# An event table of a transformer-block kernel: row maxima, one activation and the last attention results moved to other times, queues and banks

## The chip, the cores and the metric

The kernel runs on one core of a Trainium2 chip. The metric is device time in microseconds (us) of one execution, from the first to the last instruction and the little that lies around them; a kernel's time is the median of its runs. All arithmetic that the output depends on is done in the kernel.

## The reference

A block with adaptive layer norms works on x of 2048 rows and 576 columns. It has windowed attention with 32 heads of 18 columns, a token mixer with shifted rows, and an MLP of width 4608. Cut to what matters:

```python
def _A_ref(x, wqkv, wo):                       # H = 32, Dh = 18, W = 256
    q, k, v = ...                              # x @ wqkv, split into heads
    scores = jnp.einsum("bhqd,bhkd->bhqk", q, k) * (Dh ** -0.5)
    mask = (idx[:, None] - idx[None, :] >= 0) & (idx[:, None] - idx[None, :] < W)
    p = _softmax(jnp.where(mask, scores, -1e9), axis=-1)
    return (p @ v).reshape(B, S, D) @ wo       # written short

def _B_ref(x, w1, w2, w3, w4):
    h = _gelu(_layernorm(x) @ w1)
    hs = jnp.concatenate([four column groups of h, shifted by +1, -1, +2, -2 rows]) @ w2
    x1 = x + hs
    return x1 + _gelu(_layernorm(x1) @ w3) @ w4

h = _layernorm(x) * (1 + ca) + sa              # sa, ca, ga, sb, cb, gb = silu(c) @ w_mod
x = x + ga * _A_ref(h, A_wqkv, A_wo)
h = _layernorm(x) * (1 + cb) + sb
return x + gb * _B_ref(h, B_w1, B_w2, B_w3, B_w4)
```

## The kernel before

**How the order of work is set.** The class Kern does not issue its work in loops. Each piece (a function such as mtr or wom) is recorded with a time by at(t, f); build (line 1354) sorts all pieces by these times and runs them in that order, and what a piece issues lands at the end of its engines' queues. The times are only a table that orders; the chip knows nothing of them. Each engine works through its own queue in order, and an instruction waits on semaphores for what it reads and for the buffer that it writes. So a piece that is given another time stands at another place in every queue that it uses. Tiles of a pool rotate under a tag: a new tile under a tag waits until the old one's readers are done. The PSUM tags are s0 to s3 (one bank each) and m0 and m1 (two banks each).

**Stages.** qkv (projections, with q, k and v stored to DRAM), attention, mixing, mlp, each overlapping the next. A product of full precision is made of three fp32r products: an operand is split into a high part (a cast, mostly on ScalarE) and a low part (a subtraction on VectorE or GpSimd).

**Attention, head by head.** tm(h) = TA + 13 h turns heads into times; n counts 32 pairs (head groups), and u counts 16 rounds of two n, n = 2u and 2u+1. For each n, load (line 483) brings Q and K by SyncE (lines 489 and 493). mx (line 513) multiplies queries by keys once to get the row maxima; red takes them on VectorE (line 537) into the tile m. Then come three pieces that the change touches. mtr (line 543) transposes m on TensorE into the PSUM tile mt; mev (line 547) casts it on ScalarE into ms; mst (line 551) sends ms by two small DMAs into rows 108 and 109 of Q, so that the second product of queries and keys, xm (line 562, tiles X, banks s0 and s1, two matmul lines 568 and 570) comes out with the maxima subtracted. ex (line 582) takes its exponential on ScalarE into P.

**The value burst.** Once a round, av (line 593) multiplies P by V in a burst of about 230 small matmuls (line 607) into banks s2 and s3. avs (line 610) copies both banks on ScalarE, otr (line 614) transposes the copies back into s2 and s3 (tiles ot), onm (line 619) normalises on VectorE (reciprocal, line 624, and product, line 625), and ost (line 627) stores o.

**The output projection** goes by 16 row blocks t, one in each round from the sixth on: orow loads the block, otT transposes it (tiles pa, pb), otev splits it into T (casts on ScalarE, lines 678 and 679; low parts on VectorE, 680 and 681), wom multiplies by Wo in two halves (line 692), woe adds x (696), ln1 takes statistics (130 to 132), ln1n normalises in two steps (707 and 708), ln2 takes statistics again, ln2n (line 717) makes xn on ScalarE, and st1 to st3 store. wotile sets the times of blocks 0 to 9; last(te), with te = tm(34.07), those of blocks 10 to 15 and of the last round's results. The last burst, av15, has the time tm(34.05), or te - 0.26.

**The mixer's start.** mixing begins at te + 0.01, beside these last blocks: w1split casts W1 (lines 849 and 850) with low parts of slices 1 and 3 on VectorE (852, 854) and the others on GpSimd; tr transposes xn (ptm, line 895), tev splits it into xT (902 to 905), and w1mm makes the first products pg (line 916). w2split casts W2 on ScalarE (872).

Of the kernel before, what the change touches and what calls it, by code (L numbers as in the profile page):

```python
# [8 lines left out]
F32 = mybir.dt.float32  # L9
# [10 lines left out]
P = 128  # L20
# [13 lines left out]
class Kern:  # L34
# [34 lines left out]
    def at(self, t, f, *a):  # L69
        self.ev.append((t, (lambda: f(*a)) if a else f))  # L70
# [382 lines left out]
    def attention(self, t1, t2, TA, HU, LX=2.05):  # L453
        nc, at, ps = self.nc, self.at, self.ps
        X, M = {}, self.rowm
        tm = lambda h: TA + HU * h
# [84 lines left out]
                    nc.vector.tensor_reduce(out=m[:, c + s:c + s + 1], in_=pm[:, s, 320 - w:320], axis=mybir.AxisListType.X, op=ALU.max, negate=True)  # L541

        def mtr(n):
            pt = X["mt", n] = ps.tile([16, P], F32, tag="s3", name=f"mt{n}")
            nc.tensor.transpose(pt, X["m", n], self.ident)

        def mev(n):
# [3 lines left out]
        def mst(n):  # L551
            ms, Q = X["ms", n], X["Q"][n % 4]
            for r in range(2):
                nc.scalar.dma_start(Q[108 + r:109 + r].bitcast(F32), ms[:, 64 * r:64 * r + 64].bitcast(F32))

        BANKS = [[(0, 0), (5, 320)], [(-2, 0), (1, 192)], [(-4, 0), (2, 64), (6, 384)], [(-3, 0), (3, 128), (7, 448)], [(-1, 0), (4, 256)]]

# [170 lines left out]
        def wotile(t, h, b0=2):  # L728
            at(tm(h - 0.2), orow, t)
            at(tm(h + 0.42), otT, t, b0)  # L730
            at(tm(h + 0.43), otev, t)
            at(tm(h + 0.77), wom, t, 0, b0)
            at(tm(h + 0.92), woe, t, 0)
            at(tm(h + 1.15), wom, t, 1, b0)
            at(tm(h + 1.16), ln1, t, 0)
            at(tm(h + 1.30), woe, t, 1)
            at(tm(h + 1.31), ln1, t, 1)
            at(tm(h + 1.95), st1, t)
            at(tm(h + 1.712), ln1n, t)
            at(tm(h + 1.714), ln2, t)  # L740
            at(tm(h + 2.05), ln2n, t)
            at(tm(h + 2.1), st2, t)
            at(tm(h + 2.35), st3, t)

        N = 32
        for n in range(N):
            at(max(t1 + .5 + n * .01, tm(n - (0.98 if n < 12 else 0.86))), load, n)
            for j in range(2):
                at(max(t1 + .6, tm(n - 0.3 + 0.5 * j)), qs, n, j)
                for bb in range(4):  # L750
                    th = n + (4 * j + bb) / 8
                    at(tm(th), mx, n, j, bb)
                    at(tm(th + .06), red, n, j, bb)
                    if n in (1, 2):
                        at(tm(th + .01), self.warm, 2, "s3")
                at(max(t2 + .01, tm(n + LX - (0.77 if n < 12 else 0.6) + 0.47 * j)), ks, n, j)
                for k in range(5):
                    th = n + LX + (5 * j + k) / 10
                    at(tm(th), xm, n, j, k)
                    at(tm(th + .03), ex, n, j, k)  # L760
            hm = n + (1.47 if n % 2 else 1.16)
            at(tm(hm), mtr, n)
            at(tm(hm + .005), mev, n)
            at(tm(hm + .006), mst, n)
        for u in range(16):
            h = 2 * u + LX + 2
            if u == 15:
# [14 lines left out]
        for t in range(10):  # L782
            wotile(t, 12.4 + 2 * t)

        def last(te):
            for r in range(2):
                at(te + 5.0 + .01 * r, avs, 15, r)
                at(te + 9.9 + .1 * r, otr, 15, r)
                at(te + 11.4 + .1 * r, onm, 15, r)
            at(te + 13.3, ost, 15)  # L790
            for t, b0, o, a, w0, w1 in ((10, 0, -8.0, 5.02, 7.9, 11.6), (11, 2, .05, 13.6, 15.95, 17.65), (12, 2, 13.4, 19.75, 21.15, 23.2),
                                        (13, 2, 21.2, 32.1, 33.75, 35.45), (14, 2, 29.2, 37.55, 38.9, 40.6), (15, 2, 42.5, 49.85, 51.5, 53.2)):
                at(te + o, orow, t)
                at(te + a, otT, t, b0)
                at(te + a + .02, otev, t)
                for hf, w in ((0, w0), (1, w1)):
                    at(te + w, wom, t, hf, b0)
                    at(te + w + 2.05, woe, t, hf)
                e = te + w1 + 2.1
                for d, f in ((.3, ln1), (1.0, st1), (3.0, ln1n), (4.9, ln2), (5.5, st2), (7.5, ln2n), (9.5, st3)):  # L800
                    at(e + d, f, t)
# [600 lines left out]
```

## Time and profile before

| what | value |
|---|---|
| median of 3 runs | 1792.72 us (1791.35 to 1794.88) |
| profiled execution | 1794.32 us, span of its instructions 1792.5 us |
| mean granted TensorE clock over the span | 0.982 |
| busy share of the span | TensorE 94%, its weight loads 86%, VectorE 62%, GpSimd 50%, ScalarE 39% |
| 240 to 380 us, attention without a full output projection | TensorE 125.21 of 140 us, ScalarE 68.14 |
| 640 to 657 us, the last round | TensorE 14.34 of 17 us, ScalarE 11.56 |
| 657 to 690 us, last burst and the mixer's start | TensorE 27.16 of 33 us, clock 0.90 |

The profile is of one execution. In its rows PE is TensorE's matmuls, PEld its weight loads, DVE VectorE, ACT ScalarE, POOL GpSimd, SP SyncE; ACTq and SPq are the issues of DMAs from those engines' queues, which hold the queue up though they are not counted as busy. A row of a timeline gives start, duration, engine, line, operation, output <- inputs, the count where neighbours are drawn together, and in brackets how long the engine was idle before and what ended that. A row of a window gives its bounds and length, then busy time (and count) of PE, PEld, DVE, ACT, POOL, the granted clock, the DMA share and GB/s. A row of waits gives the waiting engine, tile and line, what released it, then total, count and longest. A row of groups gives busy total and mean ns of one, then the idle time before.

### The profile page before, as it was taken

How to read it: one execution, taken by the hardware profiler on the slowest of the kernel's cores; microseconds unless marked ns; L12 is line 12 of the kernel's file. 1: busy time of each engine (PE TensorE's matmuls, PEld its weight loads, DVE VectorE, ACT ScalarE, POOL GpSimd, SP SyncE). 2: the span in 40 equal slices, each digit the busy share in tenths (PEclk: the TensorE clock that was granted, in tenths of full speed). 3: DMA queues.
4: the chain of work that ended last, by engine and by line, in shares of the span. 5: the costliest groups of instructions: out<-in, count | busy, mean ns of one | idle time of the engine just before them, and what ended most of it. 6: DMA issues, size and time to landing. Idle time of an engine off the chain costs nothing.

```text
span 1792.5 us, 33622 instructions
## 1 busy us (share of the span) xinstructions
PE 1687.1 (94%) x13369; PEld 1535.6 (86%) x13369; DVE 1103.0 (62%) x1887; ACT 707.3 (39%) x1211; POOL 898.8 (50%) x837
## 2 busy tenths in 40 slices
PE   7999998999999989988799999999979999999998
PEld 5888887888989879988588999999878999999997
DVE  6544354666767636666666666666675666666664
ACT  3222144454545554444333433333433333344331
POOL 4222347445454533454766555556644556655550
PEclk9999998999999999999899999999989999999999
DMA  8854553546455446544422222211233211122211
GB/s 257 275 183 154 176 159 103 145 135 172 130 153 163 145 138 204 192 159 141 162 75 63 63 63 62 59 45 52 62 126 96 63 52 49 56 63 62 62 45 53
DMA packets 156499, 206.77 MB, mean 115 GB/s; under 512 B 19316, under 2 KB 87924, under 8 KB 155768
## 3 DMA queue, kind: packets, MB, share of 16 engines
q1 hardware_dynamic: 153720, 203.19, 36.9%
q8 instruction: 106, 1.74, 0.4%
q10 hardware_dynamic: 2624, 1.45, 0.3%
q14 instruction: 49, 0.40, 0.1%
HBM read 143.76 MB, written 60.56 MB: 114 GB/s over the span
## 4 chain that ended last, share of the span: by engine, by line
PE 73%; DVE 6%; DMA 5%; POOL 5%; issue 4%; ACT 4%; SPq 1%; ACTq 1%; POOLq 0%; DVEq 0%
PE d L1256 24%; PE qk L331 6%; PE X L568 3%; PE v L369 3%; PE mx L519 3%; PE wo L692 3%; PE av L607 3%; PE pg L916 2%; PE X L570 1%; PE w L965 1%; DVE W L1114 1%; DMA wmf<-in_w_mod_dram 1%; DMA or<-od 1%; DMA wf<-in_B_w_dram 1%; ACT avs L612 1%
## 5 line engine op out<-in xcount | busy, mean ns | idle before, releaser
L1256 PE MATMUL d<-W,G 128*128 128x288 f32 x3456 | 507.7, 297 | 12.5 <-DVE acc L1264 9.2
L1256 PEld LDWEIGHTS d<-W,G 128*128 128x128 f32 x3456 | 489.2, 189 | 34.9 <-DVE acc L1264 10.3
L1264 DVE TENSOR_TENSOR acc<-d,acc 128x576 f32<-128x576 f32 x288 | 216.9, 754 | 205.6 <-PE d L1256 203.2
L1094 POOL TENSOR_TENSOR wf<-wf 128x384 f32<-128x384 f32 x140 | 147.0, 1071 | 339.8 <-DMA wf<-in_B_w_dram 333.8
L585 ACT ACTIVATE P<-X 128x512 f32<-128x512 f32 (+4 forms) x320 | 177.8, 572 | 202.3 <-PE X L570 160.8
L537 DVE TENSOR_REDUCE m<-mx 128x2 f32<-128x640 f32 x144 | 117.8, 819 | 109.0 <-PE mx L523 108.5
L568 PE MATMUL X<-QD,KS 128*128 128x64 f32 (+2 forms) x704 | 146.2, 300 | 10.8 <-ACT P L585 9.8
L1106 POOL TENSOR_TENSOR W<-wf,W 128x768 fp32r<-128x768 f32 x70 | 152.9, 2207 | 1.2 <-ACT W L1100 1.2
L519 PE MATMUL mx<-KD,QS 128*128 128x320 f32 (+4 forms) x512 | 144.7, 342 | 7.4 <-DVE m L537 3.2
L1233 DVE TENSOR_TENSOR G<-U,G 128x512 fp32r<-128x512 f32 x108 | 88.5, 819 | 99.0 <-ACT G L1226 99.0
L499 POOL TENSOR_SCALAR QS<-QD,rowm 128x512 fp32r<-128x512 f32 x128 | 87.9, 701 | 111.6 <-DMA QD<-qd 56.4
L1224 ACT ACTIVATE U<-U 128x512 f32<-128x512 f32 x108 | 68.3, 632 | 178.3 <-DVE U L1209 178.2
L1224 ACT ACTIVATE C<-C 128x512 f32<-128x512 f32 x36 | 22.8, 632 | 286.4 <-DVE C L1209 286.4
L568 PEld LDWEIGHTS X<-QD,KS 128*128 128x128 f32 x704 | 108.6, 194 | 19.5 <-ACT P L585 16.1
L331 PE MATMUL qk<-hT,Wqk 128*128 128x512 f32 x462 | 109.3, 396 | 1.2 <-DVE qs L345 1.2
L506 POOL TENSOR_SCALAR KS<-KD,rowm 128x768 fp32r<-128x768 f32 (+1 forms) x128 | 108.5, 863 | 0.0
L1120 POOL TENSOR_TENSOR wf<-wf,gb 128x1152 f32<-128x1152 f32 x35 | 103.4, 2955 | 6.9 <-DMA wf<-in_B_w_dram 6.9
L331 PEld LDWEIGHTS qk<-hT,Wqk 128*128 128x128 f32 x462 | 86.4, 188 | 23.4 <-DVE qs L345 1.6
L519 PEld LDWEIGHTS mx<-KD,QS 128*128 128x128 f32 x512 | 93.5, 194 | 14.1 <-issue 5.3
L1135 POOL TENSOR_TENSOR W<-wf,W 128x1152 fp32r<-128x1152 f32 x35 | 96.8, 2766 | 6.9 <-ACT W L1129 6.9
L1100 ACT CAST W<-wf 128x1152 fp32r<-128x1152 f32 x70 | 90.2, 1318 | 20.5 <-DMA wf<-in_B_w_dram 10.4
L570 PE MATMUL X<-Mk,identr 128*128 128x256 f32 (+2 forms) x320 | 96.6, 302 | 0.0
(787 smaller groups left out, 3211.3 us busy)
## 6 DMA issues: line engine op xcount, KB each, us to landing
wf<-in_B_w_dram SPq DMA_DIRECT2D x35, 576.0 KB
wf<-in_B_w_dram SPq DMA_DIRECT2D x140, 128.0 KB
KD<-kd SPq DMA_DIRECT2D x72, 216.0 KB
QD<-qd SPq DMA_DIRECT2D x96, 144.0 KB
wf<-in_B_w_dram SPq DMA_DIRECT2D x140, 64.0 KB
qd<-qs SPq DMA_DIRECT2D x16, 512.0 KB
kd<-qs SPq DMA_DIRECT2D x16, 512.0 KB
vd<-Vst SPq DMA_DIRECT2D x16, 312.0 KB
```

Source lines behind the costliest of these rows:

```text
L331: nc.tensor.matmul(po, W[:, a, fs], H[:, c, :], start=(n == 0), stop=(n == 13))
L506: nc.gpsimd.tensor_scalar(t[:, b0:, r], src[:, b0:], M[:, 2 + r:3 + r], 0.0, op0=ALU.mult, op1=ALU.add)
L519: nc.tensor.matmul(pm[:, s, 320 - 64 * nb:320], lhs, K[:, j, 64 * (i + 5 - nb):64 * (i + 5)], start=True, stop=merged(n, j, bb))
L537: nc.vector.tensor_reduce(out=m[:, c:c + 2], in_=pm[:, :, 0:320], axis=mybir.AxisListType.X, op=ALU.max, negate=True)
L568: nc.tensor.matmul(px[:, c:c + q1 - q0], K[:, b + 4].rearrange("p r k -> p (r k)"), Q[:, j, q0:q1], start=(i == 0), stop=False)
L570: nc.tensor.matmul(o, self.identr, mv, start=False, stop=True)
L585: nc.scalar.activation(p[:, lo:], X["px", n, j, k][:, lo:], AF.Exp, scale=SCALE)
L1094: nc.gpsimd.tensor_tensor(out=WF[:, o], in0=WF[:, a], in1=WF[:, b], op=ALU.subtract)
L1106: eng.tensor_tensor(out=W[:, s0:s1, 3:5, :], in0=WF[:, 1 + s0:1 + s1, 0:2], in1=W[:, s0:s1, 0:2, :].bitcast(F32), op=ALU.subtract)
L1120: nc.gpsimd.tensor_tensor(out=R4, in0=R4, in1=gb.unsqueeze(1).to_broadcast([P, 2, D]), op=ALU.mult)
L1256: nc.tensor.matmul(po, G[:, g, ta, b, ts], W[:, w, b, cs], start=(n == 0), stop=(n == 5))
L1264: nc.vector.tensor_tensor(out=a, in0=po, in1=a, op=ALU.add)
```

## The change

Only places in the event table, one PSUM tag and one DMA queue change; what is computed stays as it was.

1. mtr of odd n (that is, the second of a round) stands under tag s0 instead of s3, and at n + 1.105 instead of n + 1.47: right behind the value burst instead of behind the avs copies.
2. mst issues its two DMAs from SyncE instead of ScalarE, and has the time hm + 0.14 instead of hm + 0.006, where hm is mtr's time.
3. ln2n of blocks 0 to 9 has h + 1.86 instead of h + 2.05: among the exponentials behind the burst instead of behind the avs copies.
4. In last, the results of the last round (avs, otr, onm, ost) come at te + 0.1, 0.35, 0.55 and 4.0 instead of te + 5.0, 9.9, 11.4 and 13.3; block 10's otT and otev come at te - 1.1, ahead of av15, instead of te + 5.02, and its two halves of wom at te + 0.25 and 0.5 instead of 7.9 and 11.6. Its later steps follow from these, 11.1 earlier.

```diff
 def mtr(n):
-    pt = X["mt", n] = ps.tile([16, P], F32, tag="s3", name=f"mt{n}")
+    pt = X["mt", n] = ps.tile([16, P], F32, tag="s0" if n % 2 else "s3", name=f"mt{n}")
...
-        nc.scalar.dma_start(Q[108 + r:109 + r].bitcast(F32), ms[...])
+        nc.sync.dma_start(Q[108 + r:109 + r].bitcast(F32), ms[...])
...
-    at(tm(h + 2.05), ln2n, t)
+    at(tm(h + 1.86), ln2n, t)
...
-    hm = n + (1.47 if n % 2 else 1.16)
+    hm = n + (1.105 if n % 2 else 1.16)
     at(tm(hm), mtr, n)
     at(tm(hm + .005), mev, n)
-    at(tm(hm + .006), mst, n)
+    at(tm(hm + .14), mst, n)
...
-    at(te + 5.0 + .01 * r, avs, 15, r)
-    at(te + 9.9 + .1 * r, otr, 15, r)
-    at(te + 11.4 + .1 * r, onm, 15, r)
-at(te + 13.3, ost, 15)
-for t, b0, o, a, w0, w1 in ((10, 0, -8.0, 5.02, 7.9, 11.6), ...
+    at(te + .1 + .01 * r, avs, 15, r)
+    at(te + .35 + .05 * r, otr, 15, r)
+    at(te + .55 + .05 * r, onm, 15, r)
+at(te + 4.0, ost, 15)
+for t, b0, o, a, w0, w1 in ((10, 0, -8.0, -1.1, .25, .5), ...
```

ScalarE's queue before, in the round of the twelfth burst (av11), from the first exponential behind the burst; ms25 are the row maxima of n = 25, P24 the exponentials of n = 24, xn6 the result of row block 6, QD1 the Q tile that ms goes to:

```order
L585 ACTIVATE P24_0_1_7489<-X24_0_1_7485 128x512
L585 ACTIVATE P24_0_2_7510<-X24_0_2_7500 128x512
L585 ACTIVATE P24_0_3_7524<-X24_0_3_7513 128x512
L612 COPY avs11_0_7528<-av11_0_7356 128x512
L612 COPY avs11_1_7530<-av11_1_7357 128x512
L717 ACTIVATE xn6_7540<-h6_7462,c6rs_7467 128x576
L549 CAST ms25_7544<-mt25_7542 16x128
L554 DMA QD1_1987<-ms25_7544 1x16x64 x2
L585 ACTIVATE P24_0_4_7548<-X24_0_4_7533 128x512
```

The same stretch of ScalarE's queue after the change:

```order
L549 CAST ms25_7464<-mt25_7462 16x128
L585 ACTIVATE P24_0_1_7493<-X24_0_1_7489 128x512
L717 ACTIVATE xn6_7516<-h6_7466,c6rs_7471 128x576
L585 ACTIVATE P24_0_2_7518<-X24_0_2_7506 128x512
L585 ACTIVATE P24_0_3_7532<-X24_0_3_7521 128x512
L612 COPY avs11_0_7536<-av11_0_7356 128x512
L612 COPY avs11_1_7538<-av11_1_7357 128x512
L585 ACTIVATE P24_0_4_7548<-X24_0_4_7541 128x512
```

The cast of ms25 has moved from behind the copies to the front, xn6 from behind them to between the first two exponentials, and the DMA issues have left this queue.

TensorE's queue after the change at the end of that burst; mt25 is the transposed row maxima, mx26 the next pair's product for maxima:

```order
L607 MATMUL av11_0_7356<-P23_1_3_7329,V11_5646 32x64
L607 MATMUL av11_1_7357<-P23_1_3_7329,V11_5646 32x64
L545 MATMUL mt25_7462<-ident_63,m25_7173 16x128
L519 MATMUL mx26_0_1_7478<-KD2_1992,QS26_0_7298 128x320
L523 MATMUL mx26_0_1_7478<-Mq_69,identr_64 128x2x64
L519 MATMUL mx26_0_1_7478<-KD2_1992,QS26_0_7298 128x320
L523 MATMUL mx26_0_1_7478<-Mq_69,identr_64 128x2x64
```

Before, the same transpose stood later, among the products that follow:

```order
L568 MATMUL X24_0_4_7533<-QD0_1986,KS24_0_7251 128x256 x2
L570 MATMUL X24_0_4_7533<-Mk_70,identr_64 128x128
L545 MATMUL mt25_7542<-ident_63,m25_7173 16x128
L519 MATMUL mx26_1_0_7550<-KD2_1992,QS26_1_7492 128x320
L523 MATMUL mx26_1_0_7550<-Mq_69,identr_64 128x2x64
L519 MATMUL mx26_1_0_7550<-KD2_1992,QS26_1_7492 128x320
L523 MATMUL mx26_1_0_7550<-Mq_69,identr_64 128x2x64
L617 MATMUL ot11_0_7556<-ident_63,avs11_0_7528 128x128 x4
```

The transpose of m25 has moved ahead by 25 instructions to the burst's end, ahead of the products of n = 26, and no longer stands between the copies and ot11.

VectorE's queue before, behind the last burst; W1 are the low parts of the mixer's weights, T10 those of block 10, xT0 those of the mixer's first input, wo10 the output projection of block 10, rc15 and o15 the last round's results:

```order
L852 TENSOR_TENSOR W1_9164<-w1r3_9159,W1_9164 128x512
L854 TENSOR_TENSOR W1_9164<-w1r3_9159,W1_9164 128x4x16 x2
L680 TENSOR_TENSOR T10_9231<-pa10_9224,T10_9231 128x512
L681 TENSOR_TENSOR T10_9231<-pb10_9229,T10_9231 128x128
L904 TENSOR_TENSOR xT0_9165<-ptm0_9236,xT0_9165 128x4x128
L905 TENSOR_TENSOR xT0_9165<-ptm0_9236,xT0_9165 128x128
L904 TENSOR_TENSOR xT0_9165<-ptm1_9246,xT0_9165 128x4x128
L905 TENSOR_TENSOR xT0_9165<-ptm1_9246,xT0_9165 128x128
L696 TENSOR_TENSOR xr10_9001<-wo10_0_9265,xr10_9001 128x288
L624 RECIPROCAL rc15_0_9296<-ot15_0_9282 128x16
L625 TENSOR_TENSOR o15_9295<-ot15_0_9282,rc15_0_9296 128x16x18
L624 RECIPROCAL rc15_1_9299<-ot15_1_9288 128x16
```

The same place after the change, from the last round's second half on; b10 are the statistics of block 10 and h10 its normalised rows:

```order
L852 TENSOR_TENSOR W1_9176<-w1r1_9169,W1_9176 128x512
L854 TENSOR_TENSOR W1_9176<-w1r1_9169,W1_9176 128x4x16 x2
L696 TENSOR_TENSOR xr10_9001<-wo10_0_9211,xr10_9001 128x288
L696 TENSOR_TENSOR xr10_9001<-wo10_1_9236,xr10_9001 128x288
L130 BN_STATS b10st_9275<-xr10_9001 128x6
L131 BN_STATS b10st_9275<-xr10_9001 128x6
L132 BN_AGGR b10mv_9276<-b10st_9275 128x2
L852 TENSOR_TENSOR W1_9176<-w1r3_9171,W1_9176 128x512
L854 TENSOR_TENSOR W1_9176<-w1r3_9171,W1_9176 128x4x16 x2
L707 SCALAR_TENSOR_TENSOR h10_9295<-xr10_9001,b10mv_9276,cb_2810 128x576
L708 SCALAR_TENSOR_TENSOR h10_9295<-h10_9295,b10rs_9277,sb_2809 128x576
L904 TENSOR_TENSOR xT0_9177<-ptm0_9298,xT0_9177 128x4x128
```

T10, rc15 and o15 have gone ahead of this stretch; the sums, statistics and normalisation of block 10 now stand among the low parts of W1 and ahead of xT0.

More of the change, by code (lines that the diff above doesn't have):

```diff
@@ L553, in mst @@
             for r in range(2):
-                nc.scalar.dma_start(Q[108 + r:109 + r].bitcast(F32), ms[:, 64 * r:64 * r + 64].bitcast(F32))
+                nc.sync.dma_start(Q[108 + r:109 + r].bitcast(F32), ms[:, 64 * r:64 * r + 64].bitcast(F32))
         BANKS = [[(0, 0), (5, 320)], [(-2, 0), (1, 192)], [(-4, 0), (2, 64), (6, 384)], [(-3, 0), (3, 128), (7, 448)], [(-1, 0), (4, 256)]]
@@ L786, in last @@
             for r in range(2):
-                at(te + 5.0 + .01 * r, avs, 15, r)
-                at(te + 9.9 + .1 * r, otr, 15, r)
-                at(te + 11.4 + .1 * r, onm, 15, r)
-            at(te + 13.3, ost, 15)
-            for t, b0, o, a, w0, w1 in ((10, 0, -8.0, 5.02, 7.9, 11.6), (11, 2, .05, 13.6, 15.95, 17.65), (12, 2, 13.4, 19.75, 21.15, 23.2),
+                at(te + .1 + .01 * r, avs, 15, r)
+                at(te + .35 + .05 * r, otr, 15, r)
+                at(te + .55 + .05 * r, onm, 15, r)
+            at(te + 4.0, ost, 15)
+            for t, b0, o, a, w0, w1 in ((10, 0, -8.0, -1.1, .25, .5), (11, 2, .05, 13.6, 15.95, 17.65), (12, 2, 13.4, 19.75, 21.15, 23.2),
                                         (13, 2, 21.2, 32.1, 33.75, 35.45), (14, 2, 29.2, 37.55, 38.9, 40.6), (15, 2, 42.5, 49.85, 51.5, 53.2)):
```

## The prediction

> **What bounds the kernel now.** I read the shares first, then TensorE's waits by stretch, then the timelines of three places. Busy time, and TensorE's share of the stretch from 380 to 640 us (attention) and after 830 us (the MLP, which the change leaves alone):
>
> ```profile
> PE 1687.1 (94%) x13369; PEld 1535.6 (86%) x13369; DVE 1103.0 (62%) x1887; ACT 707.3 (39%) x1211; POOL 898.8 (50%) x837
> ...
> 380.00:640.00 260.00, 245.72 (x3504) 229.95 (x3510) 182.19 (x348) 130.51 (x245) 129.48 (x190) 1.00 0.51 149
> ...
> 830.00:1792.00 962.00, 923.98 (x5563) 839.32 (x5561) 612.50 (x878) 353.78 (x491) 531.08 (x325) 0.98 0.23 70
> ```
>
> TensorE bounds the program, and its queue is in order: a microsecond comes off only where it sits idle, and an idle microsecond removed there moves all that follows. So I list its idle time. Its waits from 240 to 380 us (five rounds of two heads), from 380 to 640 (nine rounds), from 640 to 657 (the last round); total, times, longest:
>
> ```profile
> PE X L568 <- ACT P L585: 7.4, 6, 2.4
> PE mt L545 <- ACT avs L612: 4.4, 5, 1.0
> ```
>
> ```profile
> PE mt L545 <- ACT avs L612: 7.6, 9, 0.8
> ...
> PE X L568 <- ACT P L585: 1.6, 9, 0.2
> ```
>
> ```profile
> PE mt L545 <- ACT avs L612: 1.3, 1, 1.3
> PE X L568 <- ACT P L585: 0.8, 4, 0.2
> PE X L568 <- issue: 0.4, 1, 0.4
> ```
>
> All of it is for ScalarE, which is 39% busy over the span: not its load, but its order in one place per round. These rows sum to 23.5 us, the most that the attention edits can win.
>
> **The nine rounds.** ScalarE, then TensorE, behind a value burst:
>
> ```profile
> 557.66 1.09 ACT L585 ACTIVATE P<-X 128x512 f32<-128x512 f32 x2 [5.23 <-PE X L570]
> 559.16 0.60 ACT L585 ACTIVATE P<-X 128x512 f32<-128x512 f32 x1 [0.41 <-PE X L570]
> 559.66 1.07 ACT L612 COPY avs<-av 128x512 f32<-128x512 f32 x2
> 560.60 0.89 ACT L717 ACTIVATE xn<-h,c6rs 128x576 f32<-128x576 f32 x1
> 561.38 0.23 ACT L549 CAST ms<-mt 16x128 fp32r<-16x128 f32 x1
> 561.64 1.15 ACTq L554 DMA_DIRECT2D QD<-ms  x2
> 562.84 1.09 ACT L585 ACTIVATE P<-X 128x512 f32<-128x512 f32 x2 [1.23 <-issue]
> ```
>
> ```profile
> 560.78 0.28 PE L545 MATMUL mt<-ident,m 128*16 128x128 f32 x1 [0.84 <-ACT avs L612]
> ...
> 561.42 0.60 PE L617 MATMUL ot<-ident,avs 128*128 128x128 f32 x4
> ...
> 563.49 0.53 PE L568 MATMUL X<-QD,KS 128*128 128x192 f32 x2 [0.17 <-ACT P L585]
> ```
>
> mt needs bank s3, which the second avs copy frees, and the exponential at 562.84 waits for no product (its 1.23 is "issue"): it stands behind the copies, xn, ms and the two DMA issues. With the change mt stands on s0 right behind the burst (ScalarE is idle there: 5.23), its 0.10 us of TensorE merely move, the DMAs go to SyncE, and xn comes between the first two exponentials. Does ot now wait where mt did? Pitches from these rows: exponential 0.50 (559.16 to 559.66), copy 0.47 (two from 559.66 to 560.60), xn 0.78 (560.60 to 561.38). First exponential 557.76 (0.10 later, for mt), xn 558.26, then 559.04, 559.54, first copy 560.04 to about 560.6; ot goes at about 560.7. TensorE alone would bring it to 560.6, so 0.1 to 0.3 of new waiting appears. ot is 0.7 earlier than 561.42; and the exponential behind the copies starts near 561.0, so X at 563.49 loses its wait too (0.17, with the slow start of its weights about 0.3). I take 1.0 a round, 9.0 in all; bounds 0.3 (ot's wait eats the rest) and 1.1. What is late next is DVE and the loads of Q and K: both start from TensorE's own steps there and move with it.
>
> **The first five rounds.** An even head's mt, with no wo product behind it, shows the DMA issues bare:
>
> ```profile
> 320.51 1.19 ACTq L554 DMA_DIRECT2D QD<-ms  x2
> 321.75 0.87 ACT L585 ACTIVATE P<-X 128x320 f32<-128x320 f32 x2 [1.26 <-issue]
> ```
>
> ```profile
> 322.24 0.44 PE L568 MATMUL X<-QD,KS 128*128 128x320 f32 x2 [1.06 <-ACT P L585]
> ...
> 327.61 0.54 PE L519 MATMUL mx<-KD,QS 128*128 128x320 f32 x2 [0.52 <-DMA KD<-kd]
> ```
>
> ```profile
> 295.07 0.87 ACT L585 ACTIVATE P<-X 128x320 f32<-128x320 f32 x2 [1.25 <-issue]
> ```
>
> ```profile
> 312.40 0.39 PE L519 MATMUL mx<-KD,QS 128*128 128x320 f32 x1 [0.71 <-DVE m L537]
> ```
>
> Of the 7.4 for exponentials I strike 1.1 of the longest wait (2.4; only the 1.25 of its DMA issues goes, the rest is a cast of Wo) and 1.06 that comes back at 327.61, where a K load issued before the gain ends last: 5.2 left. Of the 4.4 for avs I strike the longest, 1.0, since the row at 312.40 waits for DVE whatever mt does: 3.4 left. Together 8.6; bounds 5 and 11.
>
> **The last round.** No mx product is left to fill it, so exponentials pace it: the first ot moves by about 0.3, the later ones by 0.5. The wait of 0.4 is that of the last head's X for its ms rows; with mt 3 us earlier it goes. I take 0.9 of 2.5, bounds 0 and 2. **Attention: 9.0 + 8.6 + 0.9 = 18.5 us.**
>
> **The tail.** Behind the last burst TensorE has a hole of 3.93:
>
> ```profile
> 663.23 1.43 PE L607 MATMUL av<-P,V 64*32 64x320 f32 x59 [1.91 <-issue]
> ...
> 670.38 3.73 PE L692 MATMUL wo<-Wo,T 128*128 128x288 f32 x14 [3.93 <-DVE T L680]
> ...
> 677.89 1.92 PE L916 MATMUL pg<-xT,W 128*128 128x256 f32 x14
> 679.64 2.01 PE L692 MATMUL wo<-Wo,T 128*128 128x288 f32 x14
> ```
>
> ```profile
> 664.43 0.62 ACT L849 CAST W<-w1r 128x512 fp32r<-128x512 f32 x1 [6.49 <-PE av L607]
> ```
>
> I count from the burst's end, 664.4. Now pg comes at 13.5 and the eleventh block's successor wo11 at 15.2. After the change wo10 fills 0 to 1.9, ot, wo10's second half, the ptm and pa11 transposes follow to about 6.3, and pg again waits for W1 and xT. But DVE's order has turned: it now does everything of block 10 and of o15 ahead of the low parts. Means of one, from DVE's groups between 664 and 690:
>
> ```profile
> L852 DVE TENSOR_TENSOR W<-w1r,W 128x512 fp32r<-128x512 f32 x2 | 2.9, 1432 | 17.3 <-PE ptm L895 17.3
> ...
> L708 DVE SCALAR_TENSOR_TENSOR h<-h,b10rs,sb 128x576 f32<-128x576 f32 x1 | 1.8, 1806 | 0.1
> L696 DVE TENSOR_TENSOR xr<-wo,xr 128x288 f32<-128x288 f32 x4 | 1.8, 451 | 2.0 <-PE wo L692 2.0
> L904 DVE TENSOR_TENSOR xT<-ptm,xT 128x512 fp32r<-128x512 f32 x2 | 1.4, 680 | 0.0
> L854 DVE TENSOR_TENSOR W<-w1r,W 128x64 fp32r<-128x64 f32 x4 | 1.2, 344 | 0.0
> L625 DVE TENSOR_TENSOR o<-ot,rc 128x288 f32<-128x288 f32 x2 | 0.9, 457 | 0.1
> ```
>
> It starts when the first ot is there, at 2.4. For pieces without a row I take estimates from these: 0.3 for the small L624 and L905 (a little under L854), 0.9 for L707 (two L696, its 576 columns), 1.1 for block statistics (two L696 and a short one). Then o15, 2 x (0.46 + 0.3) = 1.5; W1's second and fourth slice, 2 x (1.43 + 2 x 0.34) = 4.2; two sums of xr, 0.9; block statistics, 1.1; h10, 0.9 + 1.8 = 2.7; xT, 2 x (0.68 + 0.3) = 2.0. Sum 12.4, less about 1.4 by which 21 instructions overlap (an exponential of 0.60 is followed after 0.50, so I take 0.07 each): xT ends at 13.4. So pg starts at 13.4, as before; the filled hole buys nothing. Then T11, for wo11: on ScalarE its casts now stand behind xn10, which waits for the statistics of h10. From 13.4: statistics 1.1, three short GpSimd steps 1.2 (estimated at 0.4 each, a little over L854), xn10 0.9, a cast of W2 0.8 (xn's pitch, of the same shape), T11's casts 0.8 (L849's 0.62 and a short one), DVE's low parts 1.0 (like L904 and L905), less 0.5 of overlap: wo11 at about 18.7, so 3.5 late. The bounds are 1.5 (if L708 takes no more than L707's 0.9 and the overlap is twice as large) and 5. Second, ahead of the burst's end block 10's five transposes now take five quarters of the 0.60 that four ot took: 0.7. Third, the clock:
>
> ```profile
> 668.70:675.50 6.80, 5.12 (x23) 5.11 (x23) 4.34 (x12) 3.50 (x9) 5.57 (x7) 0.50 0.16 40
> ```
>
> After the present hole the granted clock is 0.50 for 6.8 us, and wo10 runs at half speed; by 677.89 it is whole again. After the new, longer hole (6.3 to 13.4, then again until 18.7) wo11 would start at 0.50. I take 1.7, half of a stretch of 3.4 (half of the row's 6.80), bounds 0 and 3.4. The Trainium skill (TensorE: Matmul & The Clock Gate, section "What's actually happening") has the clock halve after an idle window of about 3.4 us and return after one busy window; by that, as an estimate, the cost here is 1.7 to 3.4, and the sum would end at most 1.7 later. The trace's 3.93 us hole agrees. **Tail: 3.5 + 0.7 + 1.7 = 5.9 us lost**, bounds 1 and 9. The 1.91 "issue" inside the burst I leave as it is.
>
> **The sum.** -18.5 + 5.9 = -12.6, against the profiled execution's 1794.32 (span 1792.5 and 1.8 around it): 1781.7. The median shown, 1792.72, is 1.6 below that execution: 1780.1, and I say 1780.0. Its own range: 9 to 17 us faster, 1776 to 1784.
>
> **Rivals.** *The tail wins* (0.15): if the products of W1 wait for less than DVE's whole list, pg starts up to 4 us earlier and the hole is really filled; -18.5 - 3 = -21.5, 1771. For it: the 3.93 hole exists. Against: the sum of DVE rows. *ot takes mt's wait* (0.15): 0.3 instead of 1.0 in nine rounds, -12.6 + 6.3 = -6.3, 1786. For it: xn stands ahead of the copies. *Slower: the ms rows come late through SyncE* (0.07). They now stand behind the K loads:
>
> ```profile
> 569.27 1.36 SPq L493 DMA_DIRECT2D KD<-kd  x3
> ```
>
> ```profile
> 579.17 0.40 PE L568 MATMUL X<-QD,KS 128*128 128x320 f32 x2
> ```
>
> Issued from 570.6 to 571.8, they are needed by X at 579.17: 7.4 us. Until 7.4 it costs nothing; beyond, each us costs 16 even heads 16 us, and two us give -12.6 + 32 = +19, 1812. While SyncE waits for the cast of ms, only stores of finished blocks and a V load stand behind it in its queue. By the Trainium skill (DMA: Bandwidth & Descriptors, section "Queues, rings and completion order") a queue's descriptors are consumed in ring order, so ms would wait for K's. Against it: in the rows above K ended a wait of TensorE once, by 0.52 at 327.61, and the ms rows are needed only after the products that wait for K. *No change* (0.08): what attention gains is lost in the stages after it, to a load or GpSimd; 1792. Against: TensorE is busy 924 of 962 us there.
>
> **The numbers.** My forecast has 0.55. Less than 0.2% (3.6 us) can't be told from no change. Faster: 0.55 + 0.15 + 0.15 = 0.85; same 0.08; slower 0.07. The range 1770 to 1788 takes in the forecast with its bounds, the winning tail and ot's wait, and leaves out 0.15.
>
> **What would show it.** No wait of mt for avs, ot's wait under 0.4 a round, no DMA issues of ms on ScalarE, the last burst about 18 us earlier; then a hole of some 7 us in front of the first pg and one in front of wo11 ended by T's low part, with the clock at 0.50 there. I am wrong if pg starts under 10 us after the burst, if X waits for DMAs, or if mt's idle time reappears under another name.

## The result and the profile after

| kernel | median (range, runs) | ratio to before, 95% interval |
|---|---|---|
| before | 1792.03 us (1790.79 to 1794.88, 4) | |
| changed | 1774.12 us (1771.72 to 1778.38, 4) | 0.9897 [0.9869, 0.9925] |

The changed kernel is 17.9 us faster by the medians. Its profiled execution took 1778.38 us, 15.9 less than that of before; the difference of 2 between these two readings is the spread of single runs.

The page's first line, of the changed kernel:

```profile
PE 1680.1 (95%) x13369; PEld 1530.9 (86%) x13369; DVE 1108.0 (62%) x1887; ACT 703.6 (40%) x1211; POOL 897.3 (51%) x837
```

The span fell by 15.9 us, of which 7.0 is TensorE's busy time (1687.1 before) though it runs the same matmuls; idle time alone explains 8.9. The nine rounds show why. TensorE's waits in them after the change, from the sixth burst to the fifteenth:

```profile
PE mx L519 <- DVE m L537: 1.8, 9, 0.2
PE mx L519 <- issue: 1.7, 8, 0.2
PE av L607 <- issue: 1.5, 3, 0.8
PE X L568 <- issue: 0.2, 1, 0.2
```

No wait for ScalarE is left: mt's 7.6 and X's 1.6 are gone, and ot has not taken their place. The same stretch as windows, before and then after (the columns are length, then busy time of PE, PEld, DVE, ACT and POOL, clock, DMA share, GB/s):

```profile
380.53:636.18 255.65, 241.37 (x3338) 225.95 (x3338) 178.19 (x342) 129.82 (x243) 127.00 (x188) 1.00 0.52 151
```

```profile
374.04:616.56 242.52, 237.35 (x3338) 225.25 (x3338) 178.18 (x342) 127.91 (x243) 126.94 (x188) 1.00 0.55 158
```

With equal counts of matmuls the nine rounds are 13.1 us shorter: 9.1 less idle and 4.0 less busy time. Neighbouring matmuls overlap in these rows: each begins before the one ahead has ended. A wait breaks that. Before, the matmuls of TensorE around the wait at 560.78 that the prediction shows:

```profile
559.72 0.22 PE L570 MATMUL X<-Mk,identr 128*128 128x128 f32 x1
...
560.88 0.39 PE L519 MATMUL mx<-KD,QS 128*128 128x320 f32 x1
```

After, at the end of the same burst:

```profile
540.71 0.28 PE L545 MATMUL mt<-ident,m 128*16 128x128 f32 x1
540.74 0.40 PE L519 MATMUL mx<-KD,QS 128*128 128x320 f32 x1
```

Before, mt started 1.06 after the matmul ahead of it, with 0.84 of that called idle; the other 0.22 is the whole duration of the last matmul, which nothing overlapped. Eighteen waits (nine of mt, nine of X) at 0.22 make 4.0 us. The whole nine rounds bear this out: from start to start, the nine steps to mt that waited and the steps from ot to X are 13.3 us shorter in the changed kernel's trace, of which 9.1 was idle time. ScalarE in that round:

```profile
541.02 0.26 ACT L549 CAST ms<-mt 16x128 fp32r<-16x128 f32 x1 [4.65 <-PE mt L545]
541.92 0.60 ACT L585 ACTIVATE P<-X 128x512 f32<-128x512 f32 x1 [0.64 <-PE X L570]
542.41 0.86 ACT L717 ACTIVATE xn<-h,c6rs 128x576 f32<-128x576 f32 x1
543.17 1.07 ACT L585 ACTIVATE P<-X 128x512 f32<-128x512 f32 x2
544.13 1.08 ACT L612 COPY avs<-av 128x512 f32<-128x512 f32 x2
```

ms is cast while ScalarE is idle, and no issue of a DMA stands among these any more. Behind the last burst, TensorE and then VectorE of the changed kernel:

```profile
641.79 1.38 PE L607 MATMUL av<-P,V 64*32 64x320 f32 x51 [1.14 <-issue]
643.10 2.12 PE L692 MATMUL wo<-Wo,T 128*128 128x288 f32 x14
...
649.83 0.51 PE L916 MATMUL pg<-xT,W 128*128 128x256 f32 x2 [0.24 <-ACT xT L902]
655.60 2.93 PE L916 MATMUL pg<-xT,W 128*128 128x256 f32 x12 [5.27 <-DVE xT L904]
660.85 3.73 PE L692 MATMUL wo<-Wo,T 128*128 128x288 f32 x14 [2.33 <-DVE T L680]
664.38 2.91 PE L916 MATMUL pg<-xT,W 128*128 128x256 f32 x14
...
680.59 3.60 PE L965 MATMUL w<-W,Gm 128*128 128x288 f32 x24 [1.05 <-DVE xr L696]
```

```profile
645.69 0.26 DVE L624 RECIPROCAL rc<-ot 128x16 f32<-128x16 f32 x1 [7.66 <-PE ot L617]
...
655.47 0.28 DVE L905 TENSOR_TENSOR xT<-ptm,xT 128x128 fp32r<-128x128 f32 x1
```

The burst ends at 643.17, 21.5 us earlier than before (664.66). The first two products of pg find their operands, 6.7 after the burst; the third needs the low part of xT, which VectorE makes last in its list, and waits 5.27. wo11 waits 2.33 more for T's low part. The mixer's second product (L965) starts at 680.59, against 696.76 before. Two rows of before, with the fourteen products of pg behind wo11 first, there at full clock:

```profile
681.49 1.83 PE L916 MATMUL pg<-xT,W 128*128 128x256 f32 x14
...
696.76 3.45 PE L965 MATMUL w<-W,Gm 128*128 128x288 f32 x23 [1.22 <-DVE xr L696]
```

So 16.2 of the 21.5 us are left there, and 15.6 at the last matmul of the MLP. The clock in the hole of the changed kernel, as one window:

```profile
653.20:666.80 13.60, 8.88 (x38) 8.58 (x39) 4.80 (x11) 6.41 (x12) 8.03 (x10) 0.50 0.51 155
```

TensorE is at half clock for 13.6 us here, 8.88 of them busy, where before it was 6.8 with 5.12 busy.

### The profile page after: what moved, and what is told of

Its sections match the earlier page's. It is cut to its first block, busy times and chain, and to the rows that moved or that the text cites. A ratio compares the mean times of both kernels' runs of the same rounds, so it can differ in the third digit from the quotient of the medians.

```text
span 1776.6 us, 33655 instructions
## 1 busy us (share of the span) xinstructions
PE 1680.1 (95%) x13369; PEld 1530.9 (86%) x13369; DVE 1108.0 (62%) x1887; ACT 703.6 (40%) x1211; POOL 897.3 (51%) x837
## 4 chain that ended last, share of the span: by engine, by line
PE 78%; DVE 7%; POOL 5%; DMA 3%; ACT 3%; issue 3%; SPq 1%; POOLq 0%; DVEq 0%; ACTq 0%
PE d L1256 24%; PE qk L331 6%; PE av L607 4%; PE mx L519 4%; PE X L568 4%; PE v L369 3%; PE wo L692 3%; PE pg L916 2%; PE X L570 2%; PE w L965 1%; DVE W L1114 1%; DMA wmf<-in_w_mod_dram 1%; PE mx L523 1%; PE ot L617 1%; DMA wf<-in_B_w_dram 1%
## 5 line engine op out<-in xcount | busy, mean ns | idle before, releaser
L1256 PE MATMUL d<-W,G 128*128 128x288 f32 x3456 | 507.0, 297 | 14.6 <-DVE acc L1264 10.3
L1256 PEld LDWEIGHTS d<-W,G 128*128 128x128 f32 x3456 | 488.7, 189 | 37.1 <-DVE acc L1264 11.4
L1233 DVE TENSOR_TENSOR G<-U,G 128x512 fp32r<-128x512 f32 x108 | 96.1, 890 | 99.3 <-ACT G L1226 99.3
L1100 ACT CAST W<-wf 128x1152 fp32r<-128x1152 f32 x70 | 89.8, 1319 | 15.7 <-POOL wf L1094 7.2
```

What stands on the lines that cost most here:

```text
L1256: nc.tensor.matmul(po, G[:, g, ta, b, ts], W[:, w, b, cs], start=(n == 0), stop=(n == 5))
```

## The experiments

Eleven kernels were run, each compared with runs of before on the same chip (its median there was 1789.8 to 1792.6):

| kernel | median us | ratio, 95% interval |
|---|---|---|
| e1, attention edits only | 1767.31 | 0.9867 [0.9848, 0.9887] |
| e2, tail edits only | 1797.54 | 1.0036 [1.0023, 1.0050] |
| e3, changed, block 10's later steps late | 1767.19 | 0.9876 [0.9850, 0.9902] |
| e4, mt moved only | 1787.09 | 0.9983 [0.9960, 1.0006] |
| e5, ms DMAs on SyncE only | 1784.58 | 0.9962 [0.9946, 0.9979] |
| e6, xn moved only | 1792.30 | 1.0001 [0.9987, 1.0016] |
| e7, as e3, mixer's first input early | 1770.07 | 0.9876 [0.9857, 0.9895] |
| e8, mt and ms moved | 1763.89 | 0.9855 [0.9832, 0.9878] |
| e9, mt moved, issues behind the copies | 1771.88 | 0.9892 [0.9870, 0.9914] |
| e10, as e7, xn at its old place | 1763.40 | 0.9850 [0.9826, 0.9874] |
| e11, issues two exponentials later on ScalarE | 1783.79 | 0.9955 [0.9939, 0.9970] |

### What the tail edits cost: e1 and e2

e1 is before with edits 1 to 3 of the change; e2 is before with edit 4, the new `last`:

```diff
-    at(te + 5.0 + .01 * r, avs, 15, r)
+    at(te + .1 + .01 * r, avs, 15, r)
...
-for t, b0, o, a, w0, w1 in ((10, 0, -8.0, 5.02, 7.9, 11.6), ...
+for t, b0, o, a, w0, w1 in ((10, 0, -8.0, -1.1, .25, .5), ...
```

> The three attention edits (mt, ms DMAs, xn) with the last results and block 10 as before. Theory: in the profiled execution the attention edits had won 22 us by the last burst (21.5 at its end, and 0.7 for the five transposes now ahead of it), and the tail edits give 6 us of it back; so this kernel is some 22 us faster than before, about 1770, and 4 to 6 us faster than the changed kernel. The wait before wo10 of 3.9 us is there as before. Rival: the tail edits cost nothing and the mixer gives the 6 us back by itself when it starts earlier (its loads, GpSimd); then this kernel has the time of the changed one, 1774.

> The tail edits (last results and block 10 earlier) with the attention as before. Theory: VectorE's order behind the last burst is what costs, whatever the attention does: wo11 some 2.5 to 3.5 us later after the burst, 0.7 for the transposes, 1.7 to 3.4 for the clock: 1797, 5 us slower than before. Rival (the loss in the changed kernel came from the earlier start, not from the order): no change, 1792.

Without the tail edits the kernel takes 1767.3, 6.8 us less than the changed one by the medians, though the intervals of the two ratios overlap. e2, whose interval excludes no change, is 0.36% slower than before, 6.5 us. This agrees with the theory that the tail's order costs its 6 us with a slow attention as with a fast one; clear of noise it is shown with the slow one alone. In e2's tail stand the same two waits as in the changed kernel's:


```profile
670.54 2.93 PE L916 MATMUL pg<-xT,W 128*128 128x256 f32 x12 [5.22 <-DVE xT L904]
675.79 3.73 PE L692 MATMUL wo<-Wo,T 128*128 128x288 f32 x14 [2.32 <-DVE T L680]
```

### VectorE's order behind the burst: e3 and e7

e3 is the changed kernel with the steps of block 10 that follow wom at the times that they had before:

```diff
-    e = te + w1 + 2.1
+    e = te + (13.7 if t == 10 else w1 + 2.1)
```

> The changed kernel, with block 10's statistics, normalisation and xn back at their old times (behind the mixer's first input and behind T11). Theory: VectorE reaches xT about 4 us earlier, the wait of 5.3 in the first pg shrinks to under 2 and the wait of 2.3 before wo11 goes; wo11 about 11 us after the burst instead of 17.7; 6 us faster than the changed kernel, 1768, more if the stretch at half clock there shrinks. Rival (pg's second wait is set by GpSimd's low parts of W1 or by loads): as the changed kernel, 1774.

TensorE in e3's tail; the burst ends at 637.99:

```profile
647.77 1.76 PE L916 MATMUL pg<-xT,W 128*128 128x256 f32 x12 [2.62 <-DVE xT L904]
649.34 3.51 PE L692 MATMUL wo<-Wo,T 128*128 128x288 f32 x14
```

Two waits of 7.6 us in all have become one of 2.62, and wo11 starts 11.4 after the burst instead of 17.7. The median is 6.9 below that of the changed kernel, as forecast, though by the ratios it is less and their intervals overlap; the waits show the step more surely. The wait that was left is larger than the 2 expected. But e3 only equals e1, which has the old tail. Counted from the burst's end, L965 starts after 30.0 us in e3 and 31.1 in e1; of that 1.1 the five transposes, now ahead of the burst, take 0.7 back. e7 is e3 with the mixer's first input ahead too:

```diff
-    at(s, tr, t)
-    at(s + .3, tev, t)
+    at(s if t > 1 else T1 - 14.12 + .01 * t, tr, t)
+    at(s + .3 if t > 1 else T1 - 14.10 + .01 * t, tev, t)
```

> The changed kernel with block 10's later steps at their old times, and besides with the transposes and the split of the mixer's first input right behind the last burst, ahead of o15 and of W1's low parts on VectorE. Theory: pg no longer waits for xT; what ends last is W1's last low part, about 8 us after the burst; the wait in pg falls from 2.6 to under 1 and wo11 comes 9 to 10 us after the burst: 2 us faster than with block 10 late alone, 1765, which the times alone hardly show but the trace does. Rival (pg then waits as long for GpSimd's low parts of W1): no change against that kernel, 1767.

The trace shows the step: the waits between burst and wo11 are down to 1.42 and 0.49, and wo11 starts 10.3 after the burst. L965 starts 28.0 after it, 2.0 earlier than in e3. The time does not show it: 1770.07, with the same ratio as e3. Whether those 2 us reach the end is below what these runs can tell.

### The attention edits one by one: e4, e5, e6 and e8

```diff
-    pt = X["mt", n] = ps.tile([16, P], F32, tag="s3", name=f"mt{n}")
+    pt = X["mt", n] = ps.tile([16, P], F32, tag="s0" if n % 2 else "s3", name=f"mt{n}")
-    hm = n + (1.47 if n % 2 else 1.16)
+    hm = n + (1.105 if n % 2 else 1.16)
```

That is e4, the kernel before with edit 1 alone. e5 is the kernel before with edit 2 alone, e6 with edit 3 alone:

```diff
-    nc.scalar.dma_start(Q[108 + r:109 + r].bitcast(F32), ms[...])
+    nc.sync.dma_start(Q[108 + r:109 + r].bitcast(F32), ms[...])
-    at(tm(hm + .006), mst, n)
+    at(tm(hm + .14), mst, n)
```

```diff
-    at(tm(h + 2.05), ln2n, t)
+    at(tm(h + 1.86), ln2n, t)
```

e8 has the edits of e4 and e5.

> Only the transpose of the row maxima of odd n moved to s0 and behind the burst; ms is still sent from ScalarE, right behind its cast, and xn stands behind the copies. Theory: mt's 13 us of waiting go, but the 1.2 us of DMA issues now stand ahead of the exponentials and the copies, so that exponentials and copies come later and ot waits for the copies or X for an exponential, about 0.8 us a round: 4 to 6 us faster than before, 1787. Rival (each part brings its own share, the waits just go): 13 us and their refilling, 1777.

> Only the two DMAs of ms moved to SyncE and later; mt, xn and the tail as before. Theory: what waits for an exponential behind the DMA issues goes (6.8 us of idle time from 240 to 640 us, and some 0.2 more for each of about 15 waits), the 12 us of mt's waiting for the copies stay: 8 to 10 us faster than before, 1782. Rival (mt's waiting grows by what X no longer waits, since the copies stand behind the exponentials either way): no change, 1791.

> Only xn of blocks 0 to 9 moved ahead of the avs copies. Theory: the copies come 0.78 us later, so mt (and behind it all of TensorE) waits 0.8 us longer in each of nine rounds, while the exponential behind the copies comes when it did; X's wait of 0.17 goes: 5 us slower than before, 1796. Rival (ScalarE has the time somewhere in the round): no change, 1791.

> The transpose of the row maxima and the DMAs of ms moved, xn behind the copies as before, tail as before: the attention-only kernel without the move of xn. Theory: with mt gone from s3 nothing on TensorE waits for the copies but ot, and ScalarE is ahead there with or without xn; the exponential behind the copies starts after copies and xn in either order. So the same time as the attention-only kernel, 1767, and no wait of ot or X over 0.3 a round. Rival (the move of xn is a part of the gain, since X waits for that exponential): 5 to 9 us slower than that kernel, 1774.

e4 is not distinguishable from no change, e5 is 0.38% faster, e6 is nothing, and e8 is the whole. e5 falls short of its forecast of 8 to 10 us; from 240 to 380 us its TensorE waits 5.9 us for loads of Q and K, where before waits 0.5. ScalarE in a round of e4, with the X product that waits behind it on TensorE:

```profile
547.65 0.26 ACT L549 CAST ms<-mt 16x128 fp32r<-16x128 f32 x1 [4.58 <-PE mt L545]
547.98 1.20 ACTq L554 DMA_DIRECT2D QD<-ms  x2
549.23 1.09 ACT L585 ACTIVATE P<-X 128x512 f32<-128x512 f32 x2 [1.32 <-PE X L570]
```

```profile
549.88 0.56 PE L568 MATMUL X<-QD,KS 128*128 128x128 f32 x3 [0.41 <-ACT P L585]
```

The issues now stand ahead of the exponentials, and X waits for one of them. TensorE's waits for ScalarE in the nine rounds, in e4 and in e5:

```profile
PE X L568 <- ACT P L585: 5.7, 10, 1.3
```

```profile
PE mt L545 <- ACT avs L612: 7.6, 9, 0.8
```

Each single edit leaves one of the two waits, or makes it larger: the nine rounds shrink from 255.65 to 250.46 in e4, to 249.60 in e5, and to 241.22 in e8, more than the sum (5.2 and 6.1, against 14.4). The times show the same more strongly: by the ratios 3 us and 7 us for the single edits, 26 for both.

For e6 the expectation was wrong. ScalarE there:

```profile
555.09 0.60 ACT L585 ACTIVATE P<-X 128x512 f32<-128x512 f32 x1 [5.23 <-PE X L570]
555.58 0.86 ACT L717 ACTIVATE xn<-h,c6rs 128x576 f32<-128x576 f32 x1
...
557.30 1.08 ACT L612 COPY avs<-av 128x512 f32<-128x512 f32 x2
```

From the first exponential to the first copy it is 2.21 us, against 2.00 before (557.66 to 559.66): xn mostly fills a time in which ScalarE waited for X anyway (the 0.41 in the row of before at 559.16, and the pace of the products). So it delays the copies by 0.2 only, and mt's wait by less (0.89 against 0.84), nor does it help: e8 is as fast as e1 without it. The nine rounds even hint at a small cost beside the other edits: they take 243.70 us in e1 against 241.22 in e8, and 241.86 in e7 against 241.07 in e10 (below), pairs that differ by xn alone; the medians lie the same way, but the intervals overlap.

### Is it the issue on ScalarE, or its place? e9 and e11

e9 is e4 with the issues of odd n at their old time (first diff); e11 is the kernel before with the issues still on ScalarE, 0.14 behind mt instead of 0.006 (second):

```diff
-    at(tm(hm + .006), mst, n)
+    at(tm(hm + (.371 if n % 2 else .006)), mst, n)
```

```diff
-    at(tm(hm + .006), mst, n)
+    at(tm(hm + .14), mst, n)
```

> As the kernel with only the transpose moved, but ms's two DMA issues stay on ScalarE at their old place, behind the copies and xn, instead of ahead of the exponentials. Theory: the 1.2 us of issues hurt wherever they stand in ScalarE's queue there; the exponential behind them now ends TensorE's wait, so X waits about 0.8 in each of nine rounds where mt waited 0.84, and the nine rounds win 1 to 3 us instead of the 14 with the issues on SyncE; 2 to 5 us faster than before, 1788. Rival (only their place ahead of the exponentials was bad): nine rounds win some 12 us, the time is about 1778.

My theory fell: e9 has most of the gain (0.9892), and its nine rounds take 242.17 us, 13.5 less than before where e8 wins 14.4. The issues of even n stand in e9 where they stood, right behind their casts: from 240 to 372 us X still waits 7.1 us for exponentials, against 1.5 in e8 up to 380, which fits what e9 lacks. ScalarE in e9:

```profile
539.67 0.60 ACT L585 ACTIVATE P<-X 128x512 f32<-128x512 f32 x1 [0.41 <-PE X L570]
539.82 0.51 ACTq L554 DMA_DIRECT2D QD<-ms  x1
540.17 0.58 ACT L612 COPY avs<-av 128x512 f32<-128x512 f32 x1
540.37 0.66 ACTq L554 DMA_DIRECT2D QD<-ms  x1
540.63 0.60 ACT L612 COPY avs<-av 128x512 f32<-128x512 f32 x1
```

The issues, which stand behind copies and xn in the queue, are made beside the exponential and the copies, since ms was cast 2.3 us earlier. So I formed another theory: an issue runs beside the arithmetic queued ahead of it and costs its 1.2 us only right behind the cast that it waits for, where nothing is left ahead. e11 tests it on the kernel before, with no other edit:

> The kernel before with one edit: the two DMA issues of ms stay on ScalarE but stand two exponentials behind the cast that they wait for, instead of right behind it. Theory, from the kernel with the issues behind the copies: an issue whose input is ready is made beside ScalarE's arithmetic and holds nothing up; only right behind its own cast does it cost 1.2 us. So this kernel gains what the move to SyncE alone gained: 6 to 8 us faster than before, 1785, and no idle time of 1.2 'issue' before an exponential. Rival (an issue on ScalarE costs its 1.2 us wherever it stands): no change, 1792.

It is 0.45% faster, by the times not to be told from moving the issues to SyncE (0.38%). Its nine rounds take 252.17 us, 3.5 less than before where e5 wins 6.1; 1.1 of the difference are stalls inside bursts, the rest is open. In both X's wait for exponentials is gone there. ScalarE in e11:

```profile
553.48 0.60 ACT L585 ACTIVATE P<-X 128x512 f32<-128x512 f32 x1 [0.35 <-PE X L570]
553.55 1.15 ACTq L554 DMA_DIRECT2D QD<-ms  x2
554.77 1.09 ACT L585 ACTIVATE P<-X 128x512 f32<-128x512 f32 x2 [0.69 <-PE X L570]
```

The issue starts 0.07 after the exponential and runs beside it. What follows starts just after the issue is over (554.70), but its row names X, whose last product ends at 554.74; so whether the part of the issue that sticks out holds anything up isn't shown here.

### All of it together: e10

e10 is e7 with ln2n at its old time.

> The transposes and the DMAs of ms moved, xn at its old place; the last results early, block 10's later steps at their old times, the mixer's first input right behind the burst. Theory: xn's place is worth nothing, and the tail is worth 1 to 3 us against the old one: 1762 to 1766, no wait over 1.5 us between the last burst and wo11. Rival (the mixer and the MLP give the tail's gain back): the time of the kernel with the old tail and the two attention edits, 1764 to 1767.

1763.4, the lowest median of the study, with nearly the interval of e8, which has the old tail. Both have lower medians than the changed kernel, though the intervals of both overlap that kernel's a little; that e10's tail is worth anything against the old one isn't shown.

## Why the prediction was right

The forecast was 1780.0 in a range of 1770 to 1788; 1774.12 was measured. That lies below the forecast's own narrower range of 1776 to 1784: a gain of 17.9 us where 9 to 17 were expected. Both halves of its sum are there, with the larger one mis-sized.

**The nine rounds** were forecast at 9.0 with a bound of 1.1 a round, and brought 13.1. The mechanism was right (no wait of mt, issues off ScalarE, X without its wait), the term was too small for two reasons: I took off 0.1 to 0.3 for a new wait of ot that did not come, and I priced a wait by its idle time, with 0.3 for a slow start at X alone. From start to start each of the eighteen waits cost 0.22 more. So the 23.5 us of idle time, which I called the most that the attention edits can win, are no bound: in the nine rounds the rows sum to 9.2 and 13.1 were won. (One of the rows, 0.4, isn't a wait for ScalarE either.)

**The first five rounds** were forecast at 8.6. Up to the sixth burst the changed kernel is 6.5 us ahead (380.53 to 374.04), but kernels with the same edits of mt and ms are 7.0 (e8), 11.5 (e1) and 15.7 (e10) ahead, and e2, whose attention is that of before, is 5.9 ahead (374.66). Here stretches at half clock fall differently in each execution. From 220 to 330 us, in before, the changed kernel, e10 and e2:

```profile
220.00:330.00 110.00, 97.38 (x1028) 88.77 (x1035) 62.78 (x137) 46.53 (x101) 65.12 (x85) 0.91 0.48 135
```

```profile
220.00:330.00 110.00, 99.33 (x1126) 89.46 (x1126) 61.13 (x137) 46.02 (x101) 67.07 (x89) 0.89 0.51 144
```

```profile
220.00:330.00 110.00, 100.84 (x1196) 93.49 (x1197) 67.67 (x148) 51.84 (x113) 71.06 (x92) 0.97 0.52 149
```

```profile
220.00:330.00 110.00, 99.10 (x1150) 92.01 (x1149) 62.48 (x139) 48.10 (x105) 66.65 (x88) 0.94 0.51 145
```

The clock lost in that window, (1 - share) x 110, is 9.9, 12.1, 3.3 and 6.6 us. Set right for that, the changed kernel is 6.5 + 2.2 = 8.7 and e10 15.7 - 6.6 = 9.1 ahead, but e2, without any of the edits, is 5.9 - 3.3 = 2.6 ahead too. This is an estimate, since TensorE also idles at half clock; the edits win some 6 to 9 us here, and that 8.7 comes so close to the forecast's 8.6 is partly luck. The waits show the mechanism: from 240 to 380 us those for ScalarE fall from 11.8 to 2.4 us, but 3.5 of new ones, for GpSimd's KS and QS, have come, which the sum did not have.

**The last round** was forecast at 0.9. From the end of the fifteenth burst to that of the sixteenth the changed kernel wins 1.7 with the five transposes inside; about 0.8 of that is the shorter stall inside the burst (1.91 to 1.14), which I left out and which varies between 0.8 and 2.2 in these executions.

**The tail** was forecast to lose 5.9, the 0.7 of the transposes included; 5.9 of the burst's 21.5 us are gone at the end, and with the 0.7 ahead of it that is 6.6, as in e2 (6.5). By its steps: xT's end was put at 13.4 after the burst and came at 12.6; wo11 at 18.7 and came at 17.7. Being 2.7 later than before (15.0, from the end of the burst's last product) it lost less than the 3.5 of the sum. The clock took more: wo11's first half takes 3.73 us where it took 2.01, and the fourteen products of pg behind it 2.91 where they took 1.83, so 2.8 are lost where I took 1.7. The two errors nearly cancel, which is luck: 2.7 + 0.7 + 2.8 = 6.2, against the 5.9 of the sum. The Trainium skill (TensorE: Matmul & The Clock Gate, section "What's actually happening") would have put it, as an estimate, at 1.7 to 3.4, and the trace's 2.8 lies in that; its idle window of about 3.4 us isn't what all runs show, for in e10 the half clock comes behind a wait of 1.80 (below).

**The rivals.** That the tail would win fell with e2 and with the wait of 5.27; that ot would take mt's wait, with ot's absence from the list of waits of the nine rounds. The slower one, late ms rows through SyncE, has no X waiting for a DMA in the waits of the changed kernel from 240 us to the last burst. In e5, where the issues of odd n stand later still (n + 1.61 in the table, against n + 1.245), X waits for ms's DMA once, 0.4 from 240 to 380 us; in e1 it does once too, by 0.4. So the margin can be used up, but not by the two us that the rival took. That attention's gain would be lost afterwards did not happen: 15.6 of 16.2 reach the end.

**A sign that came true.** I had said that I am wrong if pg starts under 10 us after the burst. Its first two products do, at 6.7; the other twelve of that group come at 12.4, behind the wait for xT, so the hole is there and only this sign was worded too widely.

**What I had for a wrong reason.** Part of the argument was that ScalarE's queue has to lose the issues and xn has to go ahead of the copies. e9 and e11 show that the issues only had to leave their place behind the cast, and e6 and e8 that moving xn wins nothing. The change's first two moves are the gain; the third wins nothing and may cost a little; the fourth costs.

## What to carry to other kernels

Price a wait on TensorE from start to start, not by its idle time alone, and expect two moves that remove two waits of one round to bring more together than apart. Before a step is pulled into a hole, write down the whole list of the engine that feeds what comes behind the hole: what follows the step comes along, and here it moved the statistics of a block in front of the operand that everyone waited for. A DMA issue costs most right behind the instruction that makes its data; on the same queue, later, it won about as much time as on another queue.

## What the runs showed of the hardware

A stretch at half clock does not need a long wait. In e10 the only long wait near it is the stall of 1.80 inside the burst. In the 3.4 us ahead of the half clock TensorE was busy for 1.59, and then 3.4 us of busy TensorE run at 0.50:

```profile
632.51 1.38 PE L607 MATMUL av<-P,V 64*32 64x320 f32 x51 [1.80 <-issue]
```

```profile
630.70:634.10 3.40, 1.59 (x54) 1.41 (x53) 0.00 (x0) 0.11 (x1) 0.10 (x1) 1.00 0.23 78
634.10:637.50 3.40, 3.40 (x18) 3.40 (x17) 1.58 (x4) 3.14 (x9) 0.39 (x3) 0.50 0.70 231
```

A longer wait need not bring it: in e1 the stall in the same place is 2.19 (636.49 to 638.68), and the clock stays at 1.00 until the hole behind the burst, up to 645.0.

VectorE's subtraction of one shape takes very different times beside GpSimd's. In the changed kernel's tail, VectorE's two L852 and GpSimd's rows around them:

```profile
647.01 1.59 DVE L852 TENSOR_TENSOR W<-w1r,W 128x512 fp32r<-128x512 f32 x1
650.76 0.65 DVE L852 TENSOR_TENSOR W<-w1r,W 128x512 fp32r<-128x512 f32 x1
```

```profile
646.75 1.31 POOL L852 TENSOR_TENSOR W<-w1r,W 128x512 fp32r<-128x512 f32 x1
...
650.94 0.55 POOL L133 TENSOR_SCALAR b10rs<-b10mv 128x1 f32<-128x1 f32 x1 [1.88 <-DVE b10mv L132]
```

With GpSimd at a two-operand subtraction of its own it is 1.59, with GpSimd at a single column 0.65. A mean of such a group, as I used it, hides two cases. The other traces say more: where VectorE's subtraction overlaps GpSimd's L852 by half a microsecond or more, it takes 0.55 to 0.7 us more than the overlap. It overlaps by 1.04 here (1.59), by 1.22 in e8 (1.77), by 0.56 in e8's one before that (1.11), and by 0.62 in e10 (1.17). It is as if VectorE's stood still until GpSimd's has ended; that the two share a path is what this suggests, but not shown.
